# Two families of SBUF buffers placed at spread byte offsets within 128

## Chip, core and metric

The kernel runs on one NeuronCore of a Trainium2 chip. What counts is the device time of one execution in microseconds (us). TensorE, called PE here, does the matmuls; its weight loads are a row of their own, PEld. VectorE is DVE, ScalarE is ACT, GpSimd is POOL, and SP issues most of the transfers.

## What is computed

An attention with mixing of the heads before and after the softmax, then two feed-forward nets on its output. Cut to what matters:

```python
# attention: batch 4, 12 heads, 448 positions, head size 64
scores = einsum('bhij,hg->bgij', scale * q @ k.T, w_pre)
attn = softmax(scores)
x = (einsum('bhij,hg->bgij', attn, w_post) @ v)       # -> 1792 tokens x 768
# first net
y = ((x @ w1) * (x @ w2)) @ w3 @ w_out                # 768 -> 1024 -> 1024 -> 768
# second net
out = relu(y @ w_in) ** 2 @ moe2_w_out                # 768 -> 2048 -> 768
```

## The kernel before

The attention fills the first 465 us. Behind it the two nets run over two halves (`hf`) of 896 tokens, each half in two blocks `t` of 448 columns (`TB`). Every matrix product is done three times in single-pass fp32 (type fp32r): `mm3` (line 51) takes each operand as a high and a low part and multiplies high weights by high activations, high by low, and low by high. All matmuls of the nets come from line 55: 4344 of them, with a 128x128 block of weights that is loaded anew for each, and 448 moving columns (384 in the product `p34`, which multiplies w3 by w_out once).

The stages of a half are `l1` (x times w1 and w2, 16 units; in the second half a form with fewer products, `l1_quad`, lines 751 to 817), in the first half `p34`, then `ly` (the product of both l1 results, `ab`, times the combined weights), and twice `l3` (y times w_in, squared) and `l4` (times the last weights). What is the moving operand: in `l1` the tiles x, in `l3` the tiles y (both from `new_xy`, line 636), in `ly` the wide tiles `ab`, in `l4` the wide tiles `h`, in `p34` the parts of w_out, of which four of eight lie in wide tiles (line 603). In `l1_quad` some operands lie in two more wide tiles (line 711).

Weights come in pieces of 128 x 512 or 128 x 384. `Weights` loads a piece (line 67), ACT and DVE turn it from 64-bit to 32-bit numbers (lines 83 to 99), ACT writes the high part `wh` (line 111), and POOL, for some pieces DVE, subtracts to give the low part `wl` (line 139). `place` (line 102) takes the buffers for both: eight of each, in turn, 2048 bytes wide in each partition. The wide tiles come from `big` (line 664) and, for w_out, from line 603: ten buffers for the high parts (`bh`) and ten for the low ones (`bl`), 896 columns or 3584 bytes wide. ACT writes the high part (line 670), DVE the low one (line 672), both from a list `late` that runs ahead of a later unit. `stage` (line 528) orders all of it: ahead of each unit it issues the load of the piece six ahead, the conversion of those four and three ahead, and the subtraction of that two ahead.

Where the buffers lie is set by the order of allocation; 2048 and 3584 are multiples of 128. By the addresses of the program each `wh` and `wl` buffer starts 32 bytes past a multiple of 128 (the first ones at bytes 49056 and 65440), and each wide buffer 96 past one (from 85984 and 121824). The x and y tiles start 96 past one, too (`new_xy` has 24 columns of padding ahead of one and 48 behind another for the first block). The pieces are cut at multiples of 128 columns, so all weights blocks start 32 past, all moving operands 96 past a multiple of 128. The buffers of one family are used in this order: the first slot, then the last one and on downwards; for the wide ones, counted in the order in which the code asks for tiles, that is slot 9, 7, 6, 5, 0, 8, 4, 3, 2, 1, and so on in turn.

The attention has matmuls of the same type: the scores (lines 279 to 281) stream `kt`, which lies 64 past a multiple of 128, over weights cut from `qh` and `ql` every 440 or 472 bytes. The last product of the attention, `pv` (lines 402 to 405, fp32), streams slices of `p2` that start every 472 bytes (line 403). Line 661 splits x into parts, in slices that start every 440 bytes.

Of the kernel before, what the change touches and what calls it, by code (L numbers as in the profile page):

```python
# [10 lines left out]
R = mybir.dt.float32r  # L11
# [13 lines left out]
HT = 896  # L25
# [9 lines left out]
def fused_kernel(ctx, tc, q, k, v, w_pre, w_post, w1, w2, w3t, wo, win, wo2, eye, out):  # L35
# [24 lines left out]
    class Weights:  # L60


        def __init__(self, p, wo, nraw, ny, nf, nhi, nlo):
            self.p, self.wo, self.nraw, self.ny, self.nf, self.nhi, self.nlo = p, wo, nraw, ny, nf, nhi, nlo
            self.raw, self.yt, self.ft, self.out = {}, {}, {}, {}

        def load(self, i, src, wide):
            n = src.shape[1]
            if wide:
                t = self.p.tile([128, PW, 2], I32, tag="raw", name=f"raw{i}", bufs=self.nraw)  # L70
                nc.sync.dma_start(t[:, :n].rearrange("p n t -> p (n t)"), src.bitcast(I32))
                self.raw[i] = t[:, :n]
            else:
                t = self.p.tile([128, PW], F, tag="raw", name=f"raw{i}", bufs=self.nraw)
                nc.sync.dma_start(t[:, :n], src)
                self.ft[i] = t[:, :n]
# [25 lines left out]
        def place(self, i, dst=None):  # L102
            n = self.ft[i].shape[1]
            if dst is None:
                hi = self.p.tile([128, self.wo], R, tag="wh", name=f"wh{i}", bufs=self.nhi)[:, :n]
                lo = self.p.tile([128, self.wo], R, tag="wl", name=f"wl{i}", bufs=self.nlo)[:, :n]
                dst = hi, lo
            self.out[i] = dst

        def high(self, i):  # L110
# [34 lines left out]
    for n in range(16):  # L145
        _, ic, nr = CHUNKS[n % 4]
# [345 lines left out]
    class Moe:  # L492
        def __init__(self, wp):
            self.w = Weights(wp, PW, 4, 2, 3, 8, 8)
            self.wp = wp
            self.xy, self.late, self.acc, self.ready = {}, [[] for _ in range(4)], {}, set()
            self.units, self.wot = [], {}
            for hf in range(2):
                if hf == 0:
                    l1 = [self.l1(hf, m, s) for m in range(8) for s in range(2)]  # L500
                else:
                    l1 = [self.l1_quad(j, s) for j in range(4) for s in range(2)]
                if hf == 0:

                    wop = [self.wo_piece(c, h) for c in range(8) for h in range(2)]
                    mixed, rest = l1[:4] + wop[:6], wop[6:]
                    for i in range(8):
                        mixed.append(l1[4 + i])
                        for _ in range(1 + (i % 4 == 3)):
                            mixed.append(rest.pop(0))  # L510
                    assert not rest
                    l1 = mixed + [self.p34(m) for m in range(8)] + l1[12:]
                self.units += l1
                self.units += [self.ly(hf, n) for n in range(6)]
                for gr in range(2):
                    self.units += [self.l3(hf, 8 * gr + f) for f in range(8)]
                    self.units += [self.l4(hf, gr, e) for e in range(6)]
            self.unit_kind = [u if len(u) > 2 else None for u in self.units]
            self.units = [u[:2] for u in self.units]
            self.pieces = [s for ss, _ in self.units for s in ss]  # L520
            n = np.cumsum([0] + [len(ss) for ss, _ in self.units])
            self.at = [int(x) for x in n]
            self.keep = {
                self.at[i] + j: w12d[u[2][0], u[2][1], :, HC * j : HC * j + HC]
                for i, u in enumerate(self.unit_kind) if u for j in range(2)
            }
# [70 lines left out]
        def begin(self, ap_):  # L597
            self.ap = ap_

            for c in range(8):  # L600
                for e in range(2):
                    if c < 4:
                        t = ap_.tile([128, HT], R, tag=f"b{'hl'[e]}", name=f"wo{c}_{e}", bufs=10)
                        ts = t[:, :HC], t[:, TB : TB + HC]
                    elif c < 7:
                        ts = [ap_.tile([128, TB], R, tag="oa", name=f"wo{c}_{e}{h}", bufs=12)[:, :HC] for h in range(2)]
                    else:
                        ts = [ap_.tile([128, TB], R, tag="wx", name=f"wo{c}_{e}{h}", bufs=4)[:, :HC] for h in range(2)]
                    for h in range(2):
                        self.wot[c, h] = (*self.wot.get((c, h), ()), ts[h])  # L610
            for u in range(4, 8):
                self.load_x(0, u)
            for i in range(2):
                self.units[i][1](None, 0, slice(0, TB), self.acc[i])
# [47 lines left out]
            self.ready.add((hf, u))  # L662

        def big(self, name):
            return tuple(
                self.ap.tile([128, HT], R, tag=f"b{e}", name=f"b{e}{name}", bufs=10) for e in "hl"
            )

        def split_late(self, dst, ts, p, hi=0, lo=0):
            self.late[hi].append(lambda: nc.scalar.activation(dst[0][:, ts], p, AF.Copy))  # L670
# [282 lines left out]
def _launch(arrays):  # L953
    import concourse.bacc as bacc
    from concourse.bass_utils import run_bass_kernel_spmd as run

    nc = bacc.Bacc("TRN2", target_bir_lowering=False, num_devices=1, dynamic_dma_scratch_size=512)
    args = [
        nc.dram_tensor(n, a.shape, mybir.dt.from_np(a.dtype), kind="ExternalInput").ap()
        for n, a in arrays.items()  # L960
    ]
    out = nc.dram_tensor("out", (6, 128, NT), F, kind="ExternalOutput").ap()
    with tile.TileContext(nc) as tc:
        fused_kernel(tc, *args, out)
    r = run(nc, [arrays], core_ids=[0])
    return r.results[0]["out"]
# [35 lines left out]
```

## Time and profile before

| | us |
|---|---|
| median of 3 runs | 1338.17 |
| lowest and highest | 1336.11, 1339.07 |
| the profiled execution | 1338.59 |
| its span from first to last instruction | 1336.8 |
| PE busy in it | 1299.0 |
| DVE, ACT, POOL busy | 846.8, 708.9, 427.5 |
| mean granted share of the TensorE clock | 0.989 |

The profile is that of one execution. The span stands beside the time of the same execution, not beside the median. A busy share is a mean over stages: the attention and the nets have different limits, so each stage is read by itself, and for a matmul the distance from one start to the next says more than its recorded duration, since matmuls overlap.

### The profile page before, as it was taken

Reading aid. Unit: us, or ns where it says so; the run is one execution under the profiler, and the core shown is the slowest. Engines: PE = TensorE matmul, PEld = TensorE weight load, DVE = VectorE, ACT = ScalarE, POOL = GpSimd, SP = SyncE. Lnnn points to the kernel's source line nnn. Section 1 sums busy time; section 2 is a strip of 40 time slices with the busy share of each in tenths; the row PEclk is TensorE's granted clock in tenths of the full one; section 3 lists DMA queues with packets and bytes.
Section 4 is the critical chain, followed back from the end, with each engine's and each line's share of the span. In section 5 each row is a group of like instructions: output and inputs, shape, how many; then the busy total and the mean of one; then the engine's idle time right before and its main releaser. Section 6 shows DMA issues by size and latency. Waiting matters only on the chain.

```text
span 1336.8 us, 23589 instructions
## 1 busy us (share of the span) xinstructions
PE 1299.0 (97%) x8786; PEld 1128.9 (84%) x8786; DVE 846.8 (63%) x1397; ACT 708.9 (53%) x1534; POOL 427.5 (32%) x437
## 2 busy tenths in 40 slices
PE   5999999999999799999999999999999999999998
PEld 3677777776776688899999999999999899999998
DVE  4898788788787676643216843769566327734752
ACT  4987878787887555544224533544343225434530
POOL 1253153135221322101222322236767322322231
PEclk7999999999999899999999999999999999999999
DMA  5666476466545577765223442363311223433441
GB/s 176 180 181 184 127 204 194 138 170 202 145 123 164 165 218 213 227 177 166 67 69 109 130 119 82 116 222 98 99 60 51 71 83 106 151 95 84 128 151 52
DMA packets 99335, 183.74 MB, mean 137 GB/s; under 512 B 20949, under 2 KB 68053, under 8 KB 98773
## 3 DMA queue, kind: packets, MB, share of 16 engines
q1 hardware_dynamic: 87269, 172.21, 43.7%
q10 hardware_dynamic: 11952, 10.03, 2.2%
q8 instruction: 69, 1.13, 0.4%
q14 instruction: 45, 0.37, 0.1%
HBM read 123.22 MB, written 20.45 MB: 107 GB/s over the span
## 4 chain that ended last, share of the span: by engine, by line
PE 81%; issue 6%; ACT 4%; DMA 4%; DVE 3%; POOL 2%; SPq 0%; POOLq 0%; ACTq 0%; DVEq 0%
PE l L55 39%; PE y L55 8%; PE sp L305 7%; PE tp L361 5%; PE p L55 5%; PE pv L402 5%; PE sc L279 4%; DMA r<-s 2%; ACT p L319 1%; DMA kraw<-k 1%; POOL ql L262 1%; ACT ph L344 1%; POOL wl L139 1%; DMA qraw<-q 1%; DVE nm L311 1%
## 5 line engine op out<-in xcount | busy, mean ns | idle before, releaser
L139 POOL TENSOR_TENSOR wl<-f,wh 128x384 fp32r<-128x384 f32 (+1 forms) x144 | 167.1, 1161 | 470.3 <-ACT wh L111 450.1
L95 DVE TENSOR_SCALAR f<-y 128x384 int32<-128x384 int32 (+1 forms) x176 | 134.0, 761 | 99.8 <-ACT y L83 97.5
L305 PE MATMUL sp<-r,kpre 120*120 120x448 f32 x360 | 159.0, 564 | 4.3 <-DMA r<-s 2.5
L319 ACT ACTIVATE p<-sp,nm 120x448 f32<-120x448 f32 x180 | 113.7, 639 | 69.4 <-DVE nm L311 68.7
L55 PE MATMUL l<-bhh,wl 128*128 128x448 f32 x384 | 139.3, 363 | 0.0
L55 PE MATMUL l<-bhh,wh 128*128 128x448 f32 x384 | 138.8, 362 | 0.0
L55 PE MATMUL l<-blh,wh 128*128 128x448 f32 x384 | 138.7, 361 | 0.0
L311 DVE TENSOR_REDUCE nm<-sp 120x1 f32<-120x448 f32 x180 | 108.3, 620 | 42.4 <-PE sp L305 36.2
L361 PEld LDWEIGHTS <-ph 120*128 120x128 f16 (+1 forms) x1440 | 107.7, 99 | 30.3 <-issue 29.9
L97 DVE SCALAR_TENSOR_TENSOR f<-raw,f 128x384 int32<-128x384 int32 (+1 forms) x176 | 125.4, 712 | 5.9
L111 ACT ACTIVATE wh<-f 128x384 fp32r<-128x384 f32 (+1 forms) x160 | 90.0, 562 | 73.8 <-DVE f L97 66.9
L361 PE MATMUL tp<-kwh,ph 120*128 120x120 f16 x720 | 121.0, 218 | 4.9 <-DVE p L376 3.0
L351 DVE SCALAR_TENSOR_TENSOR pl<-p,sm,ph 120x448 f16<-120x448 f32 x180 | 123.9, 730 | 0.0
L344 ACT ACTIVATE ph<-p,sm 120x448 f16<-120x448 f32 x180 | 112.0, 682 | 15.7 <-DVE sm L339 14.7
L361 PE MATMUL tp<-kwl,ph 120*128 120x120 f16 x720 | 120.1, 217 | 0.0
L361 PE MATMUL tp<-kwh,pl 120*128 120x120 f16 x720 | 120.1, 217 | 0.0
L334 POOL TENSOR_SCALAR sm<-sm 120x2 f32<-120x2 f32 (+3 forms) x94 | 31.4, 334 | 268.5 <-ACT p L319 259.8
L279 PE MATMUL sc<-kt,qh 128*110 128x448 f32 (+1 forms) x192 | 100.1, 521 | 11.8 <-DVE kt L240 10.5
L83 ACT ACTIVATE y<-raw 128x384 f32<-128x384 f32 (+1 forms) x176 | 103.3, 587 | 2.0 <-issue 0.7
L305 PEld LDWEIGHTS sp<-r,kpre 120*120 120x120 f32 x360 | 59.0, 184 | 46.0 <-issue 21.8
L290 ACT ACTIVATE s<-sc 110x448 f32<-110x448 f32 (+1 forms) x186 | 90.3, 554 | 6.9 <-PE sc L279 5.9
L859 ACT ACTIVATE r<-l 128x448 f32<-128x448 f32 x64 | 34.9, 546 | 109.6 <-PE l L55 109.6
(618 smaller groups left out, 3218.5 us busy)
## 6 DMA issues: line engine op xcount, KB each, us to landing
r<-s SPq DMA_DIRECT2D x172, 210.0 KB
raw<-win SPq DMA_DIRECT2D x64, 384.0 KB
raw<-wo SPq DMA_DIRECT2D x48, 512.0 KB
raw<-w SPq DMA_DIRECT2D x32, 384.0 KB
kraw<-k SPq DMA_DIRECT2D x24, 448.0 KB
raw<-w3t SPq DMA_DIRECT2D x16, 512.0 KB
qraw<-q SPq DMA_DIRECT2D x35, 220.0 KB
w12d<-f ACTq DMA_DIRECT2D x32, 192.0 KB
```

The lines of the kernel that those rows point to most:

```text
L55: nc.tensor.matmul(acc, w, x, start=(first and i == 0 and j == 0), stop=(last and i == n - 1 and j == 2), skip_group_check=again,)
L83: nc.scalar.activation(y, self.raw[i][:, :, 1].bitcast(F), AF.Prelu, scale=2.0**-112, alpha=-(2.0**32))
L95: nc.vector.tensor_scalar(fi, yi, 3, None, ALU.logical_shift_left)
L97: nc.vector.scalar_tensor_tensor(fi, raw[:, :, 0], 29, fi, ALU.logical_shift_right, ALU.bitwise_or)
L139: eng.tensor_tensor(self.out[i][1], self.ft.pop(i), f32(self.out[i][0]), ALU.subtract)
L279: nc.tensor.matmul(sc[:ic], t[:, hh * ic : hh * ic + ic], self.kt[b, h // 2][:, h % 2], start=(i == 0), stop=(i == 1))
L305: nc.tensor.matmul(t[:kk], self.kpre[:kk, :kk], self.rt.pop(g)[:kk], start=True, stop=True)
L311: nc.vector.tensor_reduce(nm[:kk], self.sp[g][:kk], AX.X, ALU.max, negate=True)
L319: nc.scalar.activation(p[:kk], self.sp.pop(g)[:kk], AF.Exp, bias=self.nm.pop(g)[:kk], accum_out=self.sm[g // 2][:kk, g % 2 : g % 2 + 1],)
L344: nc.scalar.activation(self.phl[g % NP][0][:kk, :S], self.pt[g][:kk], AF.Copy, scale=self.sm[g // 2][:kk, g % 2 : g % 2 + 1])
L351: nc.vector.scalar_tensor_tensor(l, self.pt.pop(g)[:kk], self.sm[g // 2][:kk, g % 2 : g % 2 + 1], h, ALU.mult, ALU.subtract)
L361: nc.tensor.matmul(t[:, j, :, :cnt], p[:kk, j * JP : j * JP + 128], w[:kk, :, :cnt], start=(i == 0), stop=(i == 2))
```

## The change

The tiles of both families become 8 columns (32 bytes) wider, and what is used of a tile starts `k` columns into it. For the weights `k` is 0 for four buffers and 4 (16 bytes) for the next four, in turn; for the wide tiles it is 0 four times, 4 four times and 1 twice (16 and 4 bytes). The tiles for w_out come from the same new function `wide`. Nothing else is edited.

```diff
+            self.placed = 0
         def place(self, i, dst=None):
             n = self.ft[i].shape[1]
             if dst is None:
-                hi = self.p.tile([128, self.wo], R, tag="wh", name=f"wh{i}", bufs=self.nhi)[:, :n]
-                lo = self.p.tile([128, self.wo], R, tag="wl", name=f"wl{i}", bufs=self.nlo)[:, :n]
-                dst = hi, lo
+                k = 4 * (self.placed % 8 // 4)
+                self.placed += 1
+                dst = tuple(
+                    self.p.tile([128, self.wo + 8], R, tag=f"w{e}", name=f"w{e}{i}", bufs=b)[:, k : k + n]
+                    for e, b in (("h", self.nhi), ("l", self.nlo))
+                )
             self.out[i] = dst
...
                     if c < 4:
-                        t = ap_.tile([128, HT], R, tag=f"b{'hl'[e]}", name=f"wo{c}_{e}", bufs=10)
+                        t = self.wide("hl"[e], f"wo{c}_{e}")
...
         def big(self, name):
-            return tuple(
-                self.ap.tile([128, HT], R, tag=f"b{e}", name=f"b{e}{name}", bufs=10) for e in "hl"
-            )
+            return tuple(self.wide(e, f"b{e}{name}") for e in "hl")
+
+        def wide(self, e, name):
+            n = self.slots[e] = self.slots.get(e, -1) + 1
+            k = (0, 0, 0, 0, 4, 4, 4, 4, 1, 1)[n % 10]
+            return self.ap.tile([128, HT + 8], R, tag=f"b{e}", name=name, bufs=10)[:, k : k + HT]
```

## Rows read from the trace of the kernel before

**Rows 1.** The page: busy time of each engine, share of the span, instructions.
```profile
PE 1299.0 (97%) x8786; PEld 1128.9 (84%) x8786; DVE 846.8 (63%) x1397; ACT 708.9 (53%) x1534; POOL 427.5 (32%) x437
```

**Rows 2.** Stretches of the nets: us, engines' busy time (instructions), clock, DMA.
```profile
465.00:560.00 95.00, 90.60 (x445) 82.37 (x444) 64.80 (x119) 51.03 (x104) 22.02 (x20) 1.00 0.72 212
560.00:655.00 95.00, 95.00 (x527) 93.11 (x526) 36.34 (x65) 37.07 (x70) 11.94 (x11) 1.00 0.54 159
712.00:941.00 229.00, 229.00 (x1147) 214.64 (x1146) 153.69 (x205) 102.56 (x207) 82.78 (x67) 1.00 0.41 125
941.00:1050.00 109.00, 107.46 (x534) 99.33 (x533) 66.96 (x97) 43.49 (x92) 73.44 (x65) 1.00 0.23 70
1103.00:1337.00 234.00, 230.15 (x1151) 215.37 (x1149) 129.33 (x183) 91.05 (x183) 64.03 (x54) 1.00 0.36 109
```

**Rows 3.** The same for line 55 alone: PE, PEld, clock, DMA.
```profile
465.00:1337.00 872.00, 862.20 (x4344) 807.92 (x4344) 1.00 0.40 121
```

**Rows 4.** Chain of waits, 560 to 942 us: start, us, what ran, instructions.
```profile
559.85 65.00 PE p L55 x375
...
653.65 57.60 PE y L55 x288
711.25 230.40 PE l L55 x1152
```

**Rows 5.** Weight loads of the scores, line 279: ns min/median/max, first and last start.
```profile
L279 PEld LDWEIGHTS sc<-kt,qh x192: 171/175/308, 7.3 to 404.1; 128*110 128x110 f32 x144, 128*118 128x118 f32 x48
...
L279 PEld LDWEIGHTS sc<-kt,ql x192: 171/177/310, 7.4 to 404.3; 128*110 128x110 f32 x144, 128*118 128x118 f32 x48
```

**Rows 6.** Weight loads of line 55, the same columns.
```profile
L55 PEld LDWEIGHTS l<-bhh,wh x384: 187/187/188, 768.5 to 1332.2; 128*128 128x128 f32 x192
...
L55 PEld LDWEIGHTS l<-bhh,wl x384: 187/188/188, 768.9 to 1332.6; 128*128 128x128 f32 x192
```

**Rows 7.** Score matmuls in order of time: start, us, shapes.
```profile
106.02 0.36 PE L279 MATMUL sc<-kt,ql 128*110 128x448 f32 x1
106.22 0.36 PE L279 MATMUL sc<-kt,qh 128*110 128x448 f32 x1
...
106.83 0.36 PE L279 MATMUL sc<-kt,ql 128*110 128x448 f32 x1
```

**Rows 8.** Chain of waits in the attention: start, us, what ran, instructions.
```profile
62.13 0.82 PE sc L279 x4
...
64.23 2.41 PE pv L402 x48
...
78.59 1.23 PE sc L279 x6
...
143.22 2.57 PE pv L402 x48
```

**Rows 9.** Weight loads' waits after 465 us: for whom, us, times, longest.
```profile
PEld l L55 <- POOL wl L139: 2.1, 5, 0.8
...
PEld q10C L55 <- POOL wl L139: 0.3, 1, 0.3
```

**Rows 10.** Chain of waits at the end of the quads.
```profile
1038.35 0.59 ACT bhab L670
...
1038.97 0.62 DVE blab L672
...
1049.27 10.87 PE y L55 x53
```

**Rows 11.** The splits of x, line 661: ns min/median/max.
```profile
L661 POOL TENSOR_TENSOR x0l<-x0l,x0h x5: 1585/1596/1687, 424.2 to 478.4; 128x660 fp32r<-128x660 f32 x4, 128x708 fp32r<-128x708 f32 x1
...
L661 DVE TENSOR_TENSOR x0l<-x0l,x0h x3: 849/881/1734, 477.8 to 480.7; 128x660 fp32r<-128x660 f32 x2, 128x708 fp32r<-128x708 f32 x1
```

**Rows 12.** POOL's low parts in the quads, tile wl: ns min/median/max.
```profile
L139 POOL TENSOR_TENSOR wl<-S,wh x32: 1005/1022/1402, 941.5 to 1035.9; 128x384 fp32r<-128x384 f32 x32
...
L139 POOL TENSOR_TENSOR wl<-quad,wh x24: 1008/1018/1399, 938.0 to 1036.9; 128x384 fp32r<-128x384 f32 x24
```

More of the change, by code (lines that the diff above doesn't have):

```diff
@@ L496, in __init__ @@
             self.xy, self.late, self.acc, self.ready = {}, [[] for _ in range(4)], {}, set()
-            self.units, self.wot = [], {}
+            self.units, self.wot, self.slots = [], {}, {}
             for hf in range(2):
```

## The prediction, made before the change was run

> **What bounds the kernel now.** I read the page's busy line first: TensorE (PE) is busy for 1299.0 of 1336.8 us and every other engine for under two thirds [rows 1]. Then I cut the span into stages. From 465 us on the two feed-forward nets run. In the first 95 us of them PE has small gaps (90.60 busy, about 4.4 us lost), after that it is busy without a break but for 1.54 us in 941 to 1050 and the end [rows 2]. All 4344 matmuls of line 55 lie there, with a granted clock of 1.00, so at the upper level, 2.4 GHz [rows 3]. The edited buffers are used nowhere else; the attention ahead (0 to 465 us) keeps its time.
>
> What is a matmul's pace there? The chain of waits merges unbroken runs: 1152 matmuls of 448 columns in 230.40 us, 288 in 57.60 us, 375 of 384 columns in 65.00 us [rows 4]. That is 200.0, 200.0 and 173.3 ns for one. 448 columns at 2.4 GHz are 186.7 ns and 384 are 160.0 ns, so each matmul carries the same 13.3 ns more (32 clock cycles). DVE, ACT, POOL and the DMAs work beside it throughout [rows 2], and the pace doesn't move. So the change is worth what it does to these 200.0 ns, 4344 times; one nanosecond of pace is 4.3 us of time.
>
> **The change part by part.** It adds and removes no instruction, no wait and no transfer, and moves no step. It shifts addresses. By the program's addresses, before the change every weights buffer starts 32 bytes past a multiple of 128 and every moving operand of line 55 starts 96 past one, so the weights being loaded and the stream always lie 64 apart. After it the tiles are 2080 and 3616 bytes wide, each 32 past a multiple of 128, so a neighbour slot is 32 further on; `k` adds 0, 16 or 4 bytes. If the slots are handed out in the same order as now (first, then from the last one downwards), the eight weights buffers come to 32, 0, 96, 64, 48, 16, 112, 80: all different. The ten wide high buffers, numbered by `k`, lie in slots 9, 7, 6, 5, 0, 8, 4, 3, 2, 1 and come to 0, 64, 32, 0, 112, 112, 112, 80, 36, 4, the low ones to 64 more. The activations x and y, which aren't edited, stay at 96. Counted over the matmuls in program order, 2016 have a wide buffer as the moving operand, 380 of all 4344 then stream from a multiple of 128, and 447 load the next weights at the same place within 128 as the stream.
>
> *Weights at other offsets.* The score matmuls of the attention are the same kind (448 columns, same type), stream from 64, and take weights from slices 440 or 472 bytes apart, so from all sixteen multiples of 8 within 128. Their weight loads take 171 at the least and 175 or 177 ns in the median over 192 each [rows 5], for 110 or 118 columns; line 55's take 187 or 188 ns for 128 [rows 6]. Their pace: five starts in a row 0.2025 us apart in the mean (106.02 to 106.83) [rows 7], and runs of four or six in 0.82 and 1.23 us [rows 8], 0.205 each with the change to the next kind of matmul in it. So weights at any multiple of 8 cost between 0 and 5 ns more than 200.0. I take 0: the shortest score load is no longer than its fewer columns make it, and runs with a mix of offsets all take the same. Ends: 0 and 3896 matmuls (those no longer 64 apart, counted) x 5 ns = 19 us; the timeline's 2.5 ns gives 9.7 us. From below, the 13.3 ns are all that could go: 4344 x 13.3 = 58 us, but no score run, with its many distances, goes under 200 ns, so nothing is excluded but little is left.
>
> *Moving operands at other offsets.* The last product of the attention streams from slices 472 bytes apart, again all multiples of 8. Its 48 passes take 2.41 us with 110 columns and 2.57 us with 118 [rows 8]: 3.3 ns for 8 columns, which is the bare clock, with no place where a slice that runs into one more 128-byte piece would show as a jump in the sum. But that is fp32 at a slower rate per column, and 4 bytes past a multiple of 8 occurs in no row. I take 0; the ends are the rival below (380 x 13.3 ns = 5.1 us less) and the 5 ns above on 2016 matmuls (10 us more, part of the 19).
>
> *The engines that fill the buffers.* ACT writes the high parts, POOL or DVE the low ones. They are hidden behind PE but for two places. First, PE's weight loads wait for POOL's low parts: 2.1 us in five waits, 0.3 us in each of three quads [rows 9] (of the quads one stands there). Second, at the end of the quads (1037.67 to 1049.27 us) the chain runs through ACT and DVE writes of a wide buffer (0.59 and 0.62 us, four times each, the first of each in the rows) before the unbroken run of the y stage starts [rows 10]; PE itself stands still for at most 1.54 us of that [rows 2]. What do offsets do to them? The x splits of line 661 work on slices 440 bytes apart and take 1585 to 1687 ns on POOL (five of them, one with 708 columns and not 660) and 849 ns at the least, 881 in the median on DVE [rows 11]. So POOL varies by 6% at most: over the 56 subtractions of the quads at some 1.02 us [rows 12] that is 3.4 us of POOL time, where POOL is busy for 73.44 of 109 us [rows 2]. I take 0 on the path. Above, the waits of 2.1 and 0.9 us doubled and a tenth on the eight writes (4.84 us) make +3.5 us; below, all these waits gone make -4.5 us (2.1, 0.9 and 1.54).
>
> The sum is 0. The profiled execution took 1338.59 us (span 1336.8); the median of the three runs is 1338.17. My time is 1338.2.
>
> The Trainium skill speaks against the change as well: "SBUF — State Buffer", section "Who interferes with whom", says that TensorE never waits on anyone and reads its stream and its weights through two independent ports. By that rule neither the gain nor the loss below exists, and the score rows agree as far as they go.
>
> **The rivals.**
> *Faster, stream starts.* The 32 cycles might be one more 128-byte piece to read: 32 columns of 4 bytes are 128 bytes, and every line-55 stream starts 96 past a multiple of 128 and so touches 15 pieces for 14 pieces of data. For it: the surplus is exactly 32 cycles at both widths [rows 4], and no stream of this kind starts at a multiple of 128 anywhere in the trace. Against it: a fixed changeover between matmuls looks the same, and the pv sum has no jump. Price: 380 x 13.3 ns = 5.1 us, 1333.1 us.
>
> *Faster, the distance of 64 is what costs.* Then 3896 matmuls lose up to 13.3 ns: 52 us, 1286 us. The score runs speak against it: other distances, no shorter pace [rows 7, 8]. "TensorE: Matmul & The Clock Gate", section "Wait — 56ns, not 53.3ns?", in the Trainium skill gives columns over 2.4 GHz plus about 2.5 ns from start to start, measured on bf16; by it this rival would end at about 1291 us (4344 x 10.8 ns less, an estimate from that page). This trace's 13.3 ns disagrees with it for this type.
>
> *Slower, weights and stream meet.* 64 apart may be the one place where both reads never meet, and the 2.5 ns that the scores show over 200.0 may be the mean cost elsewhere. It would bite from the first matmul on, in every run of line 55, since it needs no idle engine: 3896 x 2.5 ns = 9.7 us, 1347.9 us. For it: the scores are slower by just that [rows 7]. Against: they have 110 columns of weights and waits on POOL in between, and their shortest loads are offset-blind. It decides if the surplus belongs to the offsets and not to those waits.
>
> *Slower, the suppliers.* The +3.5 us of above, if ACT, DVE and POOL slow down on odd offsets in those two places: 1341.7 us.
>
> *The change doesn't do what it says.* If the slots were handed out in another order, or high and low ended alike, offsets would coincide more often; already by the count above the wide ones have 0 twice and 112 three times. That leaves 1338.2 us as well.
>
> **How the numbers follow.** Forecast 0.55, no effect for lack of distinct offsets 0.03, stream starts 0.15, distance 0.02, meeting reads 0.20, suppliers 0.05. About 0.2% (2.7 us) is what a measurement of this kernel can tell from no change. Faster 0.17, same 0.58, slower 0.25. The range has to reach one case beyond the forecast on either side: 1333.1 and 1347.9 with 1 us for the spread of runs, so 1332 to 1349; it leaves out the distance of 64 and the 19 us end.
>
> **What would show it.** In the chain after: the runs of 1152 matmuls still in 230.4 us means the forecast. If the l stage of the second net's second product (moving wide) shrinks and the first (moving y, at 96) doesn't, it is the stream starts. If both grow, it is meeting reads: then the first product, with y at 96, should grow above all in the pieces whose weights lie at 96. If the runs stand and the time moves, look at the 4.4 us of 465 to 560 and at the eight writes of 1037 to 1049. The prediction is wrong if any fp32r matmul leaves 200.0 ns.

## The result and the profile after

The changed kernel takes 1353.55 us (median of three runs, 1352.3 to 1354.05) where the kernel before took 1338.17: a ratio of 1.0116, with an interval from 1.0093 to 1.0139. It is slower by some 15 us, above the range of the prediction. Its profiled execution took 1352.3 us with a span of 1350.5.

The page's busy line, to be held against [rows 1]: PE is busy for 15.7 us more and its weight loads (PEld) for 3.0; DVE, ACT and POOL do no more than before.

```profile
PE 1314.7 (97%) x8786; PEld 1131.9 (84%) x8786; DVE 845.0 (63%) x1397; ACT 708.3 (52%) x1534; POOL 426.5 (32%) x437
```

The chain of waits, start, us, what ran, instructions; it answers to [rows 4] (the last line is the second half's l3 and l4):

```profile
556.92 68.64 PE p L55 x382
...
654.92 58.77 PE y L55 x288
713.69 234.79 PE l L55 x1152
...
1111.90 235.00 PE l L55 x1152
```

The runs are still unbroken, so nothing new is waited for. Each matmul just starts later after the one before it: 58.77 / 288 is 204.1 ns, 234.79 / 1152 is 203.8 ns, where it was 200.0. From the first start of line 55 to the last one the nets take 884.2 us and took 867.8 (read off the starts in both traces): 16.4 us more. The slower starts are 15.9 us of it (15.3 for the matmuls of 448 columns, 0.6 for those of 384). The waits inside the nets are 1.1 us shorter, and 1.6 us come from the granted clock. Two stretches show the clock, each with the kernel before first (PE, PEld, DVE, ACT, POOL busy with instructions, then the granted clock). From 455 to 465 us the last products of the attention ran at 0.52 in the one and 0.83 in the other, and the attention ended 2.6 us sooner. From 558 to 561 us, in `p34`, it is the other way round: behind PE's wait for a low part (2.04 us before, 2.02 us after) the clock stayed at 1.00 before and fell to 0.54 after, and ten matmuls started 320 ns apart, which is 384 columns at 1.2 GHz.

```profile
455.00:465.00 10.00, 9.44 (x96) 8.93 (x96) 2.88 (x5) 1.97 (x4) 2.22 (x3) 0.52 0.73 237
...
455.00:465.00 10.00, 9.44 (x109) 8.89 (x110) 3.75 (x7) 3.39 (x7) 2.67 (x4) 0.83 0.81 250
...
558.00:561.00 3.00, 2.63 (x15) 2.63 (x16) 2.93 (x7) 2.53 (x5) 0.00 (x0) 1.00 0.64 187
...
558.00:561.00 3.00, 3.00 (x11) 3.00 (x11) 2.97 (x6) 1.67 (x3) 0.00 (x0) 0.54 0.76 247
```

Over all twelve traces the nets start between 460.8 and 465.0 us, and eight of them have the low clock in `p34`. Nothing ties it to the places: of two runs below with weights at eight places and streams at one, the weights-only run has it and the coarse one hasn't. So a few us between two whole times can be the clock; the paces of the nets are read at a clock of 1.00.

The weight loads and matmuls of line 55 after (ns min/median/max), against [rows 6]:

```profile
L55 PEld LDWEIGHTS l<-bhh,wh x384: 187/188/192, 772.0 to 1345.9; 128*128 128x128 f32 x192
L55 PE MATMUL l<-bhh,wh x384: 359/366/391, 772.2 to 1346.1; 128*128 128x448 f32 x192
...
L55 PEld LDWEIGHTS l<-bhh,wl x384: 187/188/194, 772.4 to 1346.3; 128*128 128x128 f32 x192
```

The recorded load is as long as before: the cost is not in the duration of the load. One unit of l3 shows where it is. Its stream is y, at 96 past a multiple of 128 throughout; its first nine matmuls take weights from the piece at 32, the next nine from the piece at 0 (starts, in order of time):

```profile
731.86 0.36 PE L55 MATMUL l<-y0h,wh 128*128 128x448 f32 x1
...
733.46 0.37 PE L55 MATMUL l<-y0h,wl 128*128 128x448 f32 x1
733.67 0.36 PE L55 MATMUL l<-y0h,wh 128*128 128x448 f32 x1
...
735.31 0.36 PE L55 MATMUL l<-y0h,wl 128*128 128x448 f32 x1
```

Eight steps in 1.60 us, 200 ns each, then eight in 1.64 us, 205 ns each. The stream lies at the same place throughout. Only the place of the weights differs.

The suppliers haven't moved. POOL's low parts in the quads, against [rows 12], and the loads' wait for POOL, against [rows 9]:

```profile
L143 POOL TENSOR_TENSOR wl<-S,wh x32: 1008/1026/1431, 947.5 to 1044.0; 128x384 fp32r<-128x384 f32 x32
...
PEld l L55 <- POOL wl L143: 1.9, 5, 0.8
```

### The profile page after: what moved, and what is told of

It reads as the page before. It is cut to its first block, busy times and chain, and to the rows that moved or that the text cites. A ratio compares the mean times of both kernels' runs of the same rounds, so it can differ in the third digit from the quotient of the medians.

```text
span 1350.5 us, 23589 instructions
## 1 busy us (share of the span) xinstructions
PE 1314.7 (97%) x8786; PEld 1131.9 (84%) x8786; DVE 845.0 (63%) x1397; ACT 708.3 (52%) x1534; POOL 426.5 (32%) x437
## 4 chain that ended last, share of the span: by engine, by line
PE 80%; issue 7%; ACT 5%; DVE 3%; DMA 2%; POOL 2%; SPq 0%; POOLq 0%; ACTq 0%; DVEq 0%
PE l L55 39%; PE y L55 8%; PE sp L309 6%; PE p L55 5%; PE tp L365 5%; PE pv L406 4%; PE sc L283 4%; ACT p L323 2%; ACT ph L348 1%; ACT s L294 1%; POOL wl L143 1%; DVE nm L315 1%; POOL ql L266 1%; DMA qraw<-q 1%; DMA kraw<-k 1%
```

## The experiments

What is called the pace below is the distance from the start of one matmul to the start of the next, for 448 columns, where nothing is waited for. "Distance" is the place of the weights being loaded less the place of the running stream, within 256 bytes. In the kernel before all weights lie at one place within 256 and all streams at another: weights at 160, streams at 224, distance 192.

### One half of the change each

Only the weights (`wide` allocates `HT` columns at 0 again), and only the wide buffers (`place` as before).

```diff
--- changed kernel
+++ weights only
-            k = (0, 0, 0, 0, 4, 4, 4, 4, 1, 1)[n % 10]
-            return self.ap.tile([128, HT + 8], R, tag=f"b{e}", name=name, bufs=10)[:, k : k + HT]
+            return self.ap.tile([128, HT], R, tag=f"b{e}", name=name, bufs=10)
```

> Only the weights buffers are spread over eight offsets; the wide buffers are 3584 bytes again and all streams start 96 past a multiple of 128. Theory D (the distance within 128 bytes between the weights being loaded and the running stream sets the pace; 64 gives 200.0 ns per matmul of 448 columns): every stage, l1, ly, l3 and l4 alike, runs at the paces that the changed kernel shows in l3, by the weights' place: 32: 200.2, 16: 202.3, 48: 203.5, 80: 203.6, 96: 203.7, 64: 205.1, 0: 205.5, 112: 206.4, in the mean 203.8; 4344 x 3.8 = 16 us more, about 1354. Theory W (what costs is that high and low wide parts lie apart, and weights matter only with them): 200.0 in every stage, 1338.

Measured: 1349.36 us, ratio 1.0085 (1.0065 to 1.0105). Chain of waits, ly and then l3 with l4 of the first half:

```profile
653.40 58.55 PE y L55 x288
711.95 234.51 PE l L55 x1152
```

That is 203.3 and 203.6 ns. By the place of the weights the pace is, in the mean of some 440 matmuls each: 32: 200.15, 16: 202.2, 64: 202.8, 48: 203.4, 80: 203.5, 96: 203.8, 0: 205.4, 112: 206.6. But for the place 64 these are the changed kernel's l3 values, now in ly and l4, too. Behind the 202.8 of the place 64 stand two paces: of its 49 stretches (one piece with one block of columns, in the stages with 448 columns) 30 end at 200.0 and 19 run at 206.7. The nets take 15.0 us more, 14.5 of it slower starts, against 15.9 with both families moved, so the weights alone cost nearly the whole. (The profiled execution took only 10.8 us more than that of the kernel before, since its nets started at 460.8 us and not at 465.0.) Theory W falls.

> Only the wide buffers are spread; all weights start 32 past a multiple of 128. Theory D: l1 and l3, whose streams stay at 96, at 200.0 ns; ly, l4 and the parts of p34 and the quads that stream wide buffers at about 203.5, 2016 x 3.5 = 7 us more, about 1345; streams at 4, 36, 68, 100 the slowest at about 207. Theory A (absolute places count, and weights at 32 are a good place): 200.0 everywhere but for the streams at 4 past a multiple of 16, 1339 to 1341.

Measured: 1344.80 us, ratio 1.0047 (1.0028 to 1.0065). The last unit of l3 and the first of l4, starts in order of time:

```profile
764.27 0.36 PE L55 MATMUL l<-y0h,wh 128*128 128x448 f32 x1
...
767.87 0.36 PE L55 MATMUL l<-bhh,wh 128*128 128x448 f32 x1
...
772.75 0.36 PE L55 MATMUL l<-bhh,wh 128*128 128x448 f32 x1
```

18 steps in 3.60 us, 200.0 ns, with the stream at its old place; 24 in 4.88 us, 203.3 ns, as soon as the stream is a wide buffer at a new place. Over the stages: l1 200.1 and l3 200.0, ly 203.2 to 204.2, l4 203.1 to 205.3 (204.0 in the mean); the nets 7.1 us more, where 7 were expected. So it is not the weights' place alone, nor the stream's alone: moving either one costs. The halves' slower starts (14.5 and 7.6 us) don't add up to the whole (15.9): where both move, matmuls that the one has slowed already aren't slowed by as much again.

### Uniform layouts: place or distance

Nothing is spread here. Padding in `new_xy` moves x0, y0 and all of the weights; a small tile in the other pool, allocated after the streams and filled once, moves all streams there.

```diff
--- kernel before
+++ streams at multiples of 128, weights at 64
-            for e, before, after in (("h", 24, 0), ("l", 0, 48)):
+            for e, before, after in (("h", 32, 0), ("l", 0, 48)):
...
+            nc.gpsimd.memset(ap_.tile([128, 24], F, tag="pad", name="pad"), 0.0)
```

> Nothing is spread. Padding moves every stream to a multiple of 128 and every weights buffer to 64 past one: the distance of 64 is kept, both places are new. Theory D: 200.0 ns everywhere, 1338 us. Theory A (absolute places): 203 to 206 ns, 1352 to 1364. The stream-start rival of the prediction (one more 128-byte piece for a stream that doesn't start at a multiple of 128): 186.7 ns, 58 us less, 1280.

Measured: 1345.44 us, ratio 1.0055 (1.0034 to 1.0077):

```profile
653.63 58.24 PE y L55 x288
711.88 232.48 PE l L55 x1152
```

Not 186.7, so the stream-start rival is out: streams that start at a multiple of 128 still need the 200.0 of the kernel before. But not 200.0 either: ly and l4 run at 202.2, l3 at 200.0 in its first block of columns once a unit has settled (201, 201, 198 ns in turn) and at 202.3 in its second. The two blocks lie in two pools. The first is at 0 within 256, the second at 128; the weights are at 192. Both are 64 within 128, but within 256 the distance is 192 for the one and 64 for the other. That gave the next pair of runs.

```diff
--- kernel before
+++ both less 32
-            for e, before, after in (("h", 24, 0), ("l", 0, 48)):
+            for e, before, after in (("h", 16, 0), ("l", 0, 48)):
...
+            nc.gpsimd.memset(ap_.tile([128, 8], F, tag="pad", name="pad"), 0.0)
--- kernel before
+++ weights plus 128
-            for e, before, after in (("h", 24, 0), ("l", 0, 48)):
+            for e, before, after in (("h", 24, 0), ("l", 0, 80)):
```

> Nothing is spread. Padding moves every stream and every weights buffer back by 32 bytes together (streams at 192, weights at 128 within 256), so that the weights lie 64 ahead of the stream (192 within 256) as in the kernel before, at new places. Theory D256 (the distance within 256 bytes sets the pace, and 192 is the one that gives 200.0): 200.0 ns per matmul of 448 columns in every stage, the time of the kernel before, 1338 to 1340. Theory A (absolute places): 202 to 206 ns, 1347 to 1364.

Measured: 1338.20 us, ratio 0.9990 (0.9979 to 1.0002). Everything has moved by 32 bytes, and the pace is 200.0 in every stage:

```profile
652.07 57.60 PE y L55 x288
709.67 230.40 PE l L55 x1152
```

> Nothing is spread. Streams stay where they are; all weights buffers move up by 128 bytes, so that within 128 nothing changes and within 256 the distance goes from 192 to 64. Theory D256: 202.2 ns in ly, l3 and l4, as in the stage l4 of the run with streams at multiples of 128 (distance 64 there for the right-hand pool): about 9 us more, 1348. Theory D (128 is the period): 200.0 everywhere, 1338 to 1340.

Measured: 1348.02 us, ratio 1.0069 (1.0044 to 1.0093). Within 128 nothing has moved, and yet:

```profile
656.08 58.24 PE y L55 x288
714.32 232.96 PE l L55 x1152
```

202.2 ns in every stage with 448 columns, 9 us more, as expected of a distance of 64 within 256. Together with the run before them the two show that the distance counts and the places don't, for 64 and for 192, and that 128 is not its period. A longer period than 256 isn't needed: in the kernel before, the two blocks of a wide tile lie 1792 bytes apart, so that their distances differ by 256 within 512, and both run at 200.0.

### Distance 0, and twice

```diff
--- kernel before
+++ weights at 96, as the streams
-            for e, before, after in (("h", 24, 0), ("l", 0, 48)):
+            for e, before, after in (("h", 24, 0), ("l", 0, 64)):
```

> Nothing is spread. Padding moves every weights buffer to 96 past a multiple of 128, where the streams start: distance 0 in every matmul. Theory D: 203.7 ns in every stage, as the changed kernel shows it in l3 for weights at 96: 4344 x 3.7 = 16 us more, 1354. Theory C (only variety costs, any uniform layout runs at 200.0): 1338.

Measured: 1355.43 us, ratio 1.0139 (1.0105 to 1.0172). A uniform layout is slower than the spread one, so theory C (variety costs) falls. The l3 and l4 runs of the first half and of the second:

```profile
714.38 238.08 PE l L55 x1152
...
1116.82 233.48 PE l L55 x1152
```

238.08 / 1152 is 206.67 ns, 233.48 / 1152 is 202.67 ns, with the same places and the same kind of instructions. Is that chance?

> The kernel with weights at distance 0 from the streams once more, for one look: there the first half ran at 206.7 ns and the second at 202.7 with one and the same layout. If the pace follows from the layout and the order of work alone, the stages come out at the same values again; if it also hangs on how a stretch was entered, they may swap or mix.

Measured, in one execution on another chip (1357.51 us):

```profile
716.18 238.08 PE l L55 x1152
...
1118.62 233.48 PE l L55 x1152
```

Here the same again, to the last digit. So at distance 0 there are two paces. In both executions PE runs at 206.67 ns without a stop from the l1 units behind `p34` through the quads of the second half, waits at their end, and runs at 202.67 from then on. But the program alone doesn't pick the pace. One stretch of l1, 34 matmuls behind the same wait, differs between the two executions (first and last start, the run with weights at 96 and then its repeat):

```profile
527.30 0.36 PE L55 MATMUL l<-x0h,wh 128*128 128x448 f32 x1
...
534.12 0.37 PE L55 MATMUL l<-x0h,wh 128*128 128x448 f32 x1
...
529.20 0.37 PE L55 MATMUL l<-x0h,wh 128*128 128x448 f32 x1
...
535.89 0.36 PE L55 MATMUL l<-x0h,wh 128*128 128x448 f32 x1
```

33 steps take 6.82 us (206.7 ns) in the one and 6.69 us (202.7 ns) in the other. The pace changes only at a stop or where the kind of matmul changes, so it looks as if the way in picks it; that wasn't tried apart.

### Is there a better distance?

Streams stay at 224 within 256. Weights tiles are made 64 columns wider, so that all slots lie alike within 256 (at 128, by 8 columns of padding less), and each of the eight buffers starts at a `k` of its own.

```diff
--- kernel before
+++ fine
+                k = (4, 6, 7, 8, 9, 10, 12, 14)[self.placed % 8]
+                self.placed += 1
...
-                hi = self.p.tile([128, self.wo], R, tag="wh", name=f"wh{i}", bufs=self.nhi)[:, :n]
+                    self.p.tile([128, self.wo + 64], R, tag=f"w{e}", name=f"w{e}{i}", bufs=b)[:, k : k + n]
...
-            for e, before, after in (("h", 24, 0), ("l", 0, 48)):
+            for e, before, after in (("h", 24, 0), ("l", 0, 40)):
--- fine
+++ coarse
-                k = (4, 6, 7, 8, 9, 10, 12, 14)[self.placed % 8]
+                k = (32, 52, 60, 16, 24, 40, 20, 11)[self.placed % 8]
```

> Streams stay; the eight weights buffers lie at distances of 176, 184, 188, 192, 196, 200, 208 and 216 within 256 from the stream, each for whole pieces of 12 or more matmuls. Theory D256 with 192 as one exact point: 200.0 at 192 alone, 201 to 207 at its neighbours, worse at those 4 past a multiple of 16 (about 207, like the wide streams at 4, 36, 68, 100). Theory N (192 is the middle of a good stretch): 200.0 at 188 to 196 too, or lower at one of them.

> Streams stay; the eight weights buffers lie at distances of 32, 112, 144, 224, 0, 64, 240 and 204 within 256 from the stream. D256: 64 at 202.2, 0 at 202.7 to 206.7, 240 at 203.6, the others between 202 and 207, none at or under 200.0. A theory by which 32 cycles are a collision that some distance avoids: one of them well under 200, down to 187.

Measured in one execution each (1349.73 and 1348.13 us); mean pace by distance, some 440 matmuls each, with the values of the weights-only run (240 occurs there and, at 202.9, in the coarse run):

```
distance   0     16    32    48    64    80    96    112   128   144   160
ns       203.4 206.6 204.3 202.2 201.9 203.4 202.8 204.1 203.8 202.5 205.4
distance  176   184   188   192   196   200   204   208   216   224   240
ns       204.7 204.2 203.5 200.6 204.1 201.1 204.2 204.3 203.4 202.5 203.5
```

192 has the best mean of 22 (200.15 in the weights-only run, 200.0 where all matmuls have it; the rest is what changing over between pieces costs). But these are means in a mixture, and at some distances two paces stand behind one mean. Of the 49 stretches at each distance, those at 192 and at 200 all end at 200.0. At 224, 30 end at 200.0 and 18 run at some 206.7, at 96 it is 30 and 19, at 188 it is 21 and 28; at 16 all 49 run at some 206.6. Two stretches of l3 in the coarse run, both at 224 behind a piece at 144, with the same places for weights and stream, one in each half (first and ninth start):

```profile
837.97 0.37 PE L55 MATMUL l<-y0h,wh 128*128 128x448 f32 x1
...
839.63 0.37 PE L55 MATMUL l<-y0h,wl 128*128 128x448 f32 x1
...
1278.70 0.36 PE L55 MATMUL l<-y1h,wh 128*128 128x448 f32 x1
...
1280.30 0.37 PE L55 MATMUL l<-y1h,wl 128*128 128x448 f32 x1
```

Eight steps take 1.66 us in the one (some 207 ns) and 1.60 us in the other (200 ns). So the distance doesn't fix the pace alone, and 192 isn't shown to be the only good one: whole layouts were run at 192, 64 and 0 only, and one at 200, 224 or 96 might hold 200.0 as well. No stretch settles under 200.0: these runs give no faster layout, and none of the kernels beats the one before.

### Only the high wide parts moved

A tile of 32 columns, allocated between the first high and the first low wide buffer, moves the high ones by 128 bytes.

```diff
--- kernel before
+++ high parts apart
                 for e in range(2):
                     if c < 4:
+                        if c == 0 and e == 1:
+                            nc.gpsimd.memset(ap_.tile([128, 32], F, tag="pad", name="pad"), 0.0)
```

> Of the wide buffers only the high ones move, all by the same 128 bytes; low ones, x, y and weights stay. Weights then lie 64 within 256 from a wide high stream and 192 from a wide low one. Theory P (each pair of weights load and stream has its own price): l1 and l3 at 200.0; in ly and l4 two of three matmuls stream a high part (202.2 each, as with a distance of 64 throughout) and one a low part (200.0): 201.5 in the mean, about 1341. Theory L (the pace is a state that holds only while every distance is 192; it is lost at every change): ly and l4 at 203 to 204, about 1345.

Measured: 1342.50 us, ratio 1.0027 (1.0010 to 1.0044).

```profile
655.23 58.24 PE y L55 x288
713.47 231.68 PE l L55 x1152
```

l3 stays at 200.0, ly and l4 run at 202.2. That is neither theory. A price for each pair would have given 201.5. A pace lost altogether would have given 203 or more. It is exactly the 202.2 of a distance of 64 throughout, though a third of the streams, the low ones, are at 192. In the first ly of the trace the nine intervals 205, 203, 201, 201, 202, 197, 206, 199, 206 ns repeat without change, 1820 ns in all. The same pair of operands takes 205, 201 and 206 ns in turn. So here the pace belongs to a repeating cycle of several matmuls and not to one pair, and a third of the streams at the good distance brings nothing. (The nets of the profiled execution hold two stretches at the lower clock, 3.2 us in all; the paces are read outside them.)

## Why the prediction was wrong

**The bound and its unit: right.** PE's pace times 4344 was the whole of it [rows 3, 4]. The matmuls of 448 columns, at 3.9 ns more, make 15.3 us and the 384 of p34, at 1.6 ns more, 0.6; the remaining 0.5 us of the 16.4 is the lower clock in `p34` (1.6) less the shorter waits (1.1).

**"Weights at other offsets ... I take 0": this is the step that failed.** The term was 15.9 us with the wide buffers and 14.5 on its own, in slower starts. Two readings led there. First, the score loads' durations were read as blind to offsets [rows 5]. They are, and so are those of line 55 after (187 and 188 as in [rows 6]), while the pace moved by 3.8 ns: the recorded duration of a load doesn't hold this cost, and only starts do. Second, the starts themselves were there, 202.5 ns apart in the mean [rows 7] and 205 with a change of kind in it [rows 8], for the same type and number of columns, with weights at all places. That surplus over 200.0 is of the size of the cost at mixed distances (201.9 to 203.9 ns in the spread runs); the prediction left open whether it was that or the scores' waits and their 110 columns, and took 0. No run moved the scores, so what their surplus is stays open. The argument that "runs with a mix of offsets all take the same" works the other way: a mixture has the mean price.

**The rival "weights and stream meet": the right place, a wrong size and a wrong point.** It got 0.20. Its price of 2.5 ns came from four intervals; the stages show 3.6 to 4.6, with a mean of 3.9. It also took 448 matmuls as free because they stay 64 apart within 128. The weights-plus-128 run shows that 64 and 192 are different distances. And meeting isn't what sets the price: distance 0 is dear (206.67 or 202.67 where all matmuls have it, 203.4 in the table), but 16, where the two don't lie at the same place, costs 206.6. The test that the prediction named, that l3 should grow most where weights lie at 96, came out against it: 203.8 there, 206.3 at 112 in the same stage. Within 256, though, the weights at 96 are 128 away from y and not at its place, so that test was weaker than it looked.

**The range: too short above.** The upper bound of 19 us for the same term was worked out and then left outside the range, though its 5 ns for each matmul held in the mean (3.9); 1353.6 lies between the 9.7 us case and that end.

**"Moving operands at other offsets ... I take 0": wrong as well**, 7.1 us alone, within its upper end of 10. The sum over the `pv` slices [rows 8] is of another type (fp32, with two matmul records in the trace for each call) and says nothing on this one.

**"Faster, stream starts": refuted.** Streams at multiples of 128 ran at 200.0 or 202.2 ns, not 186.7. The 32 cycles are there at every place tried, so an extra piece of 128 bytes isn't what they are.

**"The distance of 64 is what costs": refuted**, it is the other way round: moving away from the old distance costs, and none tried is better. (The 1291 us worked out beside it counts all 4344 matmuls; the rival's 3896 would give 1296.)

**The suppliers: right.** POOL's durations stand as they did, and PE's waits in the nets are 1.1 us shorter. That the change does what it says was right, too: in the weights-only run the eight buffers show paces of their own, and the one worked out to stay at 32 keeps 200.0.

The rule of the Trainium skill that spoke for no effect ("SBUF — State Buffer", section "Who interferes with whom": TensorE never waits on anyone, and has two read ports of its own) is no guide to the pace of these matmuls. Eleven layouts with the same matmuls gave 1338 to 1355 us. Whether the two reads meet in the memory or inside the engine no run here shows; the runs show that the distance of their addresses decides which paces can hold, and that at some distances there are two.

## What to carry to other kernels

Where matmuls run back to back, read their start-to-start distance to a tenth of a nanosecond, and where one stretch differs from another by a per cent, take that as a price, not as noise. Here weights and streams in single-pass fp32 are best kept at the distance that gave 200.0, for all buffers and for high and low parts alike; shifting everything together is free, spreading buffers over offsets is not, and neither is another common distance such as 0 or 64. A mean pace can hide two paces: look at single stretches before calling a layout bad. A bound from a few rows of a mixture belongs into the range at its full width.

## What was not expected of the hardware

In uniform layouts the paces are fixed values: 200.0, 202.2, 202.67 and 206.67 ns are 480, 485.3, 486.4 and 496 cycles at 2.4 GHz, so in the mean 16 cycles more in none, in one of three, in two of five, or in each of the matmuls. One layout can hold two of them in the same execution, and gives the same two on another chip.

What a distance costs is not the same in `p34`, where 384 columns are streamed: distance 192 gives 173.3 ns, distance 0 the same 173.3 (206.67 or 202.67 with 448 columns), and distance 64 gives 174.7.
